# Moving the last head's output weights behind most of its V, and aligning the load buffers to 512 bytes, in a decode attention and MLP kernel

## The chip, the cores and the metric

The kernel runs on one core of a Trainium2 chip. The metric is the device time of one execution in microseconds (us). The profile's own span is 1.8 us shorter than the time (201.4 us for a run of 203.22 before). All runs quoted are at a granted TensorE clock of 1.00.

## The reference, cut to what matters

One token passes through layernorm, grouped-query attention over a cache of 16,384 keys, a residual, and an MLP. With one token there is almost no arithmetic; nearly all the work is reading the caches and weights, 79 MB (before, the load queue takes 96.2% of the DMA engines' time).

```python
# D = 512; Hq, Hkv, Sk, Dh = 32, 8, 16384, 128; everything bf16
h   = x + attention(layernorm(x), k_cache, v_cache, wq, wo)  # K and V: 33.6 MB each; wq and wo: 4.2 MB each
x1  = layernorm(h)        # B's first half adds nothing: its shifts leave only padding for a single position
out = h + x1 + gelu(layernorm(x1) @ w3) @ w4                 # w3 and w4: 1.8 MB each
```

## The kernel before

For each of the 8 KV heads, SyncE (SP) issues two K halves (2 MB), wo (512 KB) and four V quarters (1 MB). VectorE transposes K; TensorE computes scores, the softmax denominator, PV (the softmax weights times V) and the projection with wo; after the last head the MLP runs. All large loads go through one queue, issued in program order. A load waits at the issuing engine until its buffer is free, and everything behind it waits too: in the trace of before nothing is issued from 156.4 to 175.28 us, while wo waits.

```python
sb = lambda name, shape, dt: ctx.enter_context(nc.sbuf_tensor(name, shape, dt))
...                                             # some 25 small tensors, then the load buffers
wo_sb = sb("wo_sb", [128, REP, D], BF16)        # so this one starts at byte 22304 of a partition, 32 mod 256
w3_sb = ...; w4_sb = ...; wq_sb = ...           # all sizes are multiples of 512 bytes:
kraw  = [sb(f"kraw{i}", [128, HALF], BF16) for i in range(NKR)]   # every buffer behind wo_sb starts
vslot = [sb(f"vslot{a}", [128, QTR], BF16)[:, :] for a in range(NQ)]  # at 32 mod 256 as well
...
def load_v(g, a):       # free once PV of quarter a of the head before is done
    P.dma("sp", vslot[a], src, P.at(f"pv{a}", g - 1), sig=f"v{a}")
def load_wo(g):         # free once the projection of the head before is done
    P.dma("sp", wo_sb[:, :, :], wo_in[:, REP * g:REP * (g + 1), :], P.at("proj", g - 1), sig="wo")
...
for g in range(G):
    if g + 1 < G:
        load_k(g + 1, 0)
        load_k(g + 1, 1)
    load_wo(g)
    for a in range(NQ):
        load_v(g, a)
    ...
# behind the last head: w3, then w4 in four pieces
t_w3 = P.dma("sp", w3_sb[:, :, :], w3_in, sig="w3")
t_w4 = [P.dma("sp", w4_sb[:, m0:m1, :], w4_in[:, m0:m1, :], ...) for m0, m1 in W4_CUTS]
```

A load becomes packets of one contiguous run per partition: 16 KB for K, 32 KB for wq, 8 KB for V, 14 KB for w3, 1 KB for wo and w4 (in the trace of before 2,048 packets of 16 KB, 128 of 32, 4,096 of 8, 128 of 14 and 5,888 of 1). They are spread over 16 DMA engines, 768 packets an engine on average (12,288 in all).

The softmax here doesn't subtract the row's maximum and nothing guards it: scores larger than these inputs give would overflow.

## Time and profile before

| | before |
|---|---|
| time, median of 3 (range) | 203.35 us (203.06 to 203.5) |
| HBM read | 79.17 MB, 393 GB/s over the span |
| DMA engines' share, q1 | 96.2% |
| VectorE busy | 124.7 us (62%) |
| one head, from one head's last V landing to the next's | 21.28 us |

The page of the profile, its slices (40 equal parts of the span: the DMA engines' busy tenths, and what they moved) and its queue lines (packets, MB, share of 16 engines' time):

```profile
DMA  6998999999999999999999999999999999099993
GB/s 221 462 462 364 436 433 384 415 441 423 386 419 441 423 397 415 418 434 423 395 421 433 436 384 421 434 434 384 421 431 433 394 415 405 29 360 423 436 351 100
...
q1 hardware_dynamic: 13288, 79.17, 96.2%
q8 instruction: 4, 0.07, 0.1%
...
HBM read 79.17 MB, written 0.00 MB: 393 GB/s over the span
```

The DMA engines are at 9 tenths nearly throughout, but slice 35 moves only 29 GB/s. The next view gives stretches of the trace: the first is steady work, the second the hole. The last two columns are the DMA share and GB/s.

```profile
core 0: us, PE busy (x) PEld busy (x) DVE busy (x) ACT busy (x) POOL busy (x), PEclk, DMA share, GB/s
96.00:160.00 64.00, 26.51 (x822) 24.99 (x822) 44.66 (x13) 3.86 (x27) 0.00 (x0) 1.00 1.02 419
171.00:176.60 5.60, 3.83 (x130) 3.65 (x128) 1.45 (x3) 0.00 (x0) 0.00 (x0) 1.00 0.13 35
```

In the steady stretch the DMA engines are always busy (1.02; the records of packets overlap a little, with 16.2 in flight on average) at 419 GB/s. In the hole they are at 0.13. The time line of the issuing engine shows why (start, duration, engine, line, what; "x4" are four issues in a row):

```profile
154.43 1.94 SPq L71 DMA_DIRECT2D vslot<-in_A_v_cache_dram  x4
175.28 0.38 SPq L71 DMA_DIRECT2D wo_sb<-in_A_wo_dram  x1
175.70 1.93 SPq L71 DMA_DIRECT2D vslot<-in_A_v_cache_dram  x4
```

Nothing is issued between 156.4 and 175.28 us. The time line of TensorE tells what the issue waits for (idle before and its releaser in brackets):

```profile
165.79 1.02 PE L283 MATMUL ot_ps<-p_sb,vslot 128*128 128x4 bf16 x32 [6.43 <-DMA vslot<-in_A_v_cache_dram]
168.27 1.02 PE L283 MATMUL ot_ps<-p_sb,vslot 128*128 128x4 bf16 x32 [1.46 <-DMA vslot<-in_A_v_cache_dram]
170.76 1.01 PE L283 MATMUL ot_ps<-p_sb,vslot 128*128 128x4 bf16 x32 [1.47 <-DMA vslot<-in_A_v_cache_dram]
173.23 1.02 PE L283 MATMUL ot_ps<-p_sb,vslot 128*128 128x4 bf16 x32 [1.46 <-DMA vslot<-in_A_v_cache_dram]
174.56 0.69 PE L290 MATMUL h_ps<-OT,wo_sb 128*128 128x1 bf16 x16 [0.31 <-DVE OT L315]
...
189.01 1.02 PE L283 MATMUL ot_ps<-p_sb,vslot 128*128 128x4 bf16 x32 [1.47 <-DMA vslot<-in_A_v_cache_dram]
```

The four V slots are free after each of the first four groups, at 166.8, 169.3, 171.8 and 174.3 us. But wo stands ahead of them and waits for the projection, which ends at 175.25. The chain that ended last shows the same loop, and the end of the kernel:

```profile
155.93 17.25 DMA vslot<-in_A_v_cache_dram
...
173.23 1.03 PE ot_ps L283 x32
...
174.56 0.70 PE h_ps L290 x16
...
175.28 0.38 SPq L71
...
190.45 8.06 DMA w_sb<-in_B_w_dram
...
198.55 0.41 PE qr_ps L371 x8
...
199.06 0.29 DVE fin L375
```

In the other heads K loads fill the queue meanwhile; the last head has no K to load. After the last V comes the end: w3 and w4 land (the last piece at 198.51 us), and TensorE finishes with it.

Two more readings of the trace, which no view prints, come from its single packet and completion records. (1) From 2 to 171.06 us, 16 packets are in flight without a gap; from 171.06 to 176.54 us, 1.7 on average. (2) A load completes 16 times, and the core has 16 DMA engines: a completion is read here as one engine's, though the records do not name it. The last V of head 6 completes on its first engine at 171.44 us and on its last at 173.18, a spread of 1.74 us. The last V of head 7, behind the hole, completes from 188.51 to 188.96, a spread of 0.45 us.

### The profile page before, as it was taken

What the parts mean: (1) busy time and instruction counts of PE and PEld (TensorE: products, weight loads), DVE (VectorE), ACT (ScalarE), POOL (GpSimd) and SP (SyncE); (2) the same over time, 40 slices, a digit from 0 to 9 for tenths busy, and PEclk for the clock granted to TensorE, in tenths of its full rate; (3) what the DMA queues carried; (4) which work ended last, traced back from release to release, by engine and by line L of the source; (5) the groups of instructions that cost most, each with busy time, mean ns of one, the idle gap of its engine ahead of it and who ended that gap; (6) DMA issues with size and microseconds to landing.
All of it is one profiled execution on the core that took longest, in us unless ns stands there. A gap on an engine that the chain in (4) does not pass through costs nothing.

```text
span 201.4 us, 5325 instructions
## 1 busy us (share of the span) xinstructions
PE 80.3 (40%) x2473; PEld 75.1 (37%) x2473; DVE 124.7 (62%) x69; ACT 17.5 (9%) x85; POOL 0.5 (0%) x5
## 2 busy tenths in 40 slices
PE   0104307344724560467044812491247304664554
PEld 0004206233713550366033802391137303653452
DVE  2186692997399649943995199709990699200030
ACT  2030002000200020002000100002000200040040
POOL 0000000000000000000000000000000000000000
PEclk9999999999999999999999999999999999999999
DMA  6998999999999999999999999999999999099993
GB/s 221 462 462 364 436 433 384 415 441 423 386 419 441 423 397 415 418 434 423 395 421 433 436 384 421 434 434 384 421 431 433 394 415 405 29 360 423 436 351 100
DMA packets 13438, 79.26 MB, mean 394 GB/s; under 512 B 1144, under 2 KB 7032, under 8 KB 7032
## 3 DMA queue, kind: packets, MB, share of 16 engines
q1 hardware_dynamic: 13288, 79.17, 96.2%
q8 instruction: 4, 0.07, 0.1%
q10 hardware_dynamic: 144, 0.00, 0.0%
q14 instruction: 2, 0.02, 0.0%
HBM read 79.17 MB, written 0.00 MB: 393 GB/s over the span
## 4 chain that ended last, share of the span: by engine, by line
DMA 55%; DVE 12%; SPq 12%; PE 11%; issue 7%; ACT 1%; DVEq 0%
DMA vslot<-in_A_v_cache_dram 42%; SPq L71 12%; DVE kt L240 11%; DMA wq_sb<-in_A_wq_dram 8%; DMA w_sb<-in_B_w_dram 4%; PE s_ps L274 4%; PE ot_ps L283 3%; PE h_ps L290 2%; PE q_ps L229 2%; ACT p_sb L263 1%; DVE OT L315 1%; PE den_ps L278 1%; DVE Qbd L251 0%; DVEq L90 0%; PE qr_ps L371 0%
## 5 line engine op out<-in xcount | busy, mean ns | idle before, releaser
L240 DVE STREAM_TRANSPOSE kt<-kraw 128x4096 f32<-128x4096 f32 x16 | 117.5, 7409 | 30.3 <-PE s_ps L274 30.3
L283 PE MATMUL ot_ps<-p_sb,vslot 128*128 128x4 bf16 x1024 | 32.6, 169 | 73.5 <-DMA vslot<-in_A_v_cache_dram 73.5
L283 PEld LDWEIGHTS ot_ps<-p_sb,vslot 128*128 128x128 bf16 x1024 | 29.8, 104 | 76.2 <-DMA vslot<-in_A_v_cache_dram 76.2
L274 PE MATMUL s_ps<-Qcur,kt 128*128 128x16 bf16 x1024 | 28.5, 174 | 8.4 <-DVE kt L240 8.4
L274 PEld LDWEIGHTS s_ps<-Qcur,kt 128*128 128x128 bf16 x1024 | 28.0, 104 | 8.5 <-issue 8.5
L263 ACT ACTIVATE p_sb<-s_ps 128x128 bf16<-128x128 f32 x32 | 8.4, 277 | 146.3 <-PE s_ps L274 146.3
L315 DVE TENSOR_TENSOR OT<-ot_ps,rden 128x4 bf16<-128x4 f32 x8 | 1.3, 163 | 19.1 <-PE ot_ps L283 18.7
L278 PE MATMUL den_ps<-accden,ones_f 128*128 128x4 f32 x16 | 4.5, 349 | 10.6 <-ACT p_sb L263 10.6
L278 PEld LDWEIGHTS den_ps<-accden,ones_f 128*128 128x128 f32 x16 | 4.0, 310 | 11.1 <-issue 11.1
L290 PE MATMUL h_ps<-OT,wo_sb 128*128 128x1 bf16 x128 | 5.5, 173 | 5.7 <-DVE OT L315 5.7
L290 PEld LDWEIGHTS h_ps<-OT,wo_sb 128*128 128x128 bf16 x128 | 4.9, 118 | 6.4 <-DVE OT L315 6.4
L229 PE MATMUL q_ps<-xn,wq_sb 128*128 128x1 bf16 x128 | 3.6, 165 | 8.4 <-DMA wq_sb<-in_A_wq_dram 8.4
L229 PEld LDWEIGHTS q_ps<-xn,wq_sb 128*128 128x128 bf16 x128 | 3.5, 104 | 8.5 <-issue 8.5
L263 ACT ACTIVATION_READ_ACCUMULATOR p_sb<-s_ps 128x1 f32 x32 | 6.6, 207 | 0.0
L314 DVE RECIPROCAL rden<-den_ps 128x4 f32<-128x4 f32 x8 | 1.2, 154 | 6.2 <-PE den_ps L278 6.2
L206 PE MATMUL den_ps<-ln,mean_f 128*128 128x8 f32 x4 | 1.1, 357 | 9.6 <-DVE ln L204 9.0
L206 PEld LDWEIGHTS den_ps<-ln,mean_f 128*128 128x128 f32 x4 | 1.0, 312 | 9.6 <-issue 9.6
L203 DVE CAST ln<-xcol 128x4 f32<-128x4 bf16 x1 | 0.2, 170 | 5.8 <-DMA xcol<-in_A_x_dram 5.8
L257 ACT ACTIVATE Qcur<-Qbd 128x64 bf16<-128x64 bf16 x8 | 2.2, 270 | 11.2 <-DVE Qbd L251 11.2
L375 DVE CAST fin<-qr_ps 128x128 bf16<-128x128 f32 x1 | 0.3, 292 | 4.3 <-PE qr_ps L371 4.3
L371 PE MATMUL qr_ps<-w_sb,hcol 128*1 128x128 bf16 x56 | 2.2, 303 | 0.4 <-DMA w_sb<-in_B_w_dram 0.4
L244 DVE CAST QT<-q_ps 128x32 bf16<-128x32 f32 x1 | 0.2, 192 | 3.2 <-PE q_ps L229 3.2
(52 smaller groups left out, 21.2 us busy)
## 6 DMA issues: line engine op xcount, KB each, us to landing
kraw<-in_A_k_cache_dram SPq DMA_DIRECT2D x16, 2048.0 KB, 18.6
vslot<-in_A_v_cache_dram SPq DMA_DIRECT2D x32, 1024.0 KB, 13.2
wq_sb<-in_A_wq_dram SPq DMA_DIRECT2D x1, 4096.0 KB, 16.7
wo_sb<-in_A_wo_dram SPq DMA_DIRECT2D x8, 512.0 KB, 9.2
w_sb<-in_B_w_dram SPq DMA_DIRECT2D x1, 1792.0 KB, 15.6
w_sb<-in_B_w_dram SPq DMA_DIRECT2D x1, 640.0 KB, 17.0
w_sb<-in_B_w_dram SPq DMA_DIRECT2D x1, 512.0 KB, 18.1
w_sb<-in_B_w_dram SPq DMA_DIRECT2D x1, 384.0 KB, 16.8
```

The costliest lines, as they stand in the source:

```text
L71: self.lists[engine].append((waits, lambda e: e.dma_start(out, in_), (token[0], 16)))
L206: t = P.op(pe, lambda e: e.matmul(den_ps[:, 0:2 * NCH], mean_f[:, :], ln[:, :], start=True, stop=True), t, t_mean, sig="stats")
L229: t_q = P.op("pe", lambda e, h=h, k=k: e.matmul(q_ps[:, h:h + 1], wq_sb[:, k, h * DH:(h + 1) * DH], xn[:, k:k + 1], start=(k == 0), stop=( ...
L240: k_free[n] = P.op("dve", lambda e: e.transpose(dst, src), k_land[n], P.at("qk", g - 1), sig=f"kt{hf}")
L257: P.op("act", lambda e: e.activation(Qcur[:, :], Qbd[:, 64 * g:64 * (g + 1)], ACTF.Copy), t_qbd, P.at("qk", g - 1), sig="qcur")
L263: P.op("act", lambda e, h=h: e.activation(p_sb[:, h * 128:(h + 1) * 128], src[:, h, :], ACTF.Exp, scale=float(SCALE), accum_out=accden[:, ...
L274: P.op("pe_loop", lambda e, J=J, l=lhs, be=be: e.matmul(s_ps[:, 16 * J:16 * J + 16], l, Qcur[:, 16 * be:16 * be + 16], start=(be == 0), st ...
L278: P.op("pe_loop", lambda e: e.matmul(den_ps[:, 0:REP], ones_f[:, :], accden[:, :], start=True, stop=True), "exp", sig="den")
L283: P.op("pe_loop", lambda e, J=J, a=a: e.matmul(ot_ps[:, 0:REP], vslot[a][:, J * DH:(J + 1) * DH], pv[:, J * NQ + a, :], start=(a == 0 and ...
L290: P.op("pe_loop", lambda e, h=h, k=k, l=lhs: e.matmul(h_ps[:, k:k + 1], l, OT[:, h:h + 1], start=False, stop=(h == REP - 1), skip_group_ch ...
L315: P.op("dve", lambda e: e.tensor_tensor(OT[:, :], ot_ps[:, 0:REP], rden[:, :], ALU.mult), P.at("pv3", g), t_rden, P.at("proj", g - 1), sig ...
L371: t = P.op("pe_tail", lambda e, m=m, q=q: e.matmul(row_ps[32 * q:32 * q + 1, 0:128], hcol[:, m:m + 1], w4_sb[:, m, 128 * q:128 * (q + 1)], ...
```

## The change

Two intents: do not let wo of the last head hold up V, and start every load buffer at a multiple of 512 bytes.

```diff
+        big = lambda name, shape, dt: ctx.enter_context(nc.sbuf_tensor(name, shape, dt, align_bytes=512))
...
-        wo_sb = sb("wo_sb", [128, REP, D], BF16)
+        wo_sb = big("wo_sb", [128, REP, D], BF16)
         (the same for w3_sb, w4_sb, wq_sb, kraw and vslot)
...
             if g + 1 < G:
                 load_k(g + 1, 0)
                 load_k(g + 1, 1)
-            load_wo(g)
+                load_wo(g)
             for a in range(NQ):
+                if g == G - 1 and a == NQ - 1:
+                    load_wo(g)
                 load_v(g, a)
```

The first load buffer moves from byte 22304 to 22528 of its partition, the others by the same 224 bytes. On SP wo of the last head moves behind three V quarters. Among the loads nothing else changes. (`kt`, into which VectorE transposes K, lies between these buffers and moves by 224 bytes as well.)

More of the change, by code (lines that the diff above doesn't have):

```diff
@@ L142, in bass_sequential_preLN__gqa_block_cached__mixer_s_mlp__decode_kernel @@
         hcol = sb("hcol", [128, NHC], BF16)
-        wo_sb = sb("wo_sb", [128, REP, D], BF16)
-        w3_sb = sb("w3_sb", [128, NCH, FM], BF16)
-        w4_sb = sb("w4_sb", [128, NHC, D], BF16)
-        wq_sb = sb("wq_sb", [128, NCH, HQ * DH], BF16)
-        kraw = [sb(f"kraw{i}", [128, HALF], BF16) for i in range(NKR)]
+        wo_sb = big("wo_sb", [128, REP, D], BF16)
+        w3_sb = big("w3_sb", [128, NCH, FM], BF16)
+        w4_sb = big("w4_sb", [128, NHC, D], BF16)
+        wq_sb = big("wq_sb", [128, NCH, HQ * DH], BF16)
+        kraw = [big(f"kraw{i}", [128, HALF], BF16) for i in range(NKR)]
         kt = sb("kt", [128, 2 * HALF], BF16)
-        vslot = [sb(f"vslot{a}", [128, QTR], BF16)[:, :] for a in range(NQ)]
+        vslot = [big(f"vslot{a}", [128, QTR], BF16)[:, :] for a in range(NQ)]
         s_ps = ps("s_ps", [128, 512], FP32)
```

## The prediction

> **What bounds the kernel now.** The DMA engines. The page's slices show DMA at 9 tenths in nearly every slice, 79.17 MB read at 393 GB/s over a 201.4 us span; DVE is second (62%, 117.5 us of it transposes). From the trace's packet records, 16 packets (one per DMA engine) are in flight without a break from 2 us to 171.06 us: a head takes 21.27 us. The chain of waits from head 2 on runs through issue, V, PV, OT and projection, but K loads fill the DMA queue meanwhile. The DVE side would allow about 19.4 us per head (transposes end at 172.3, OT waits until 174.3).
>
> The one hole is the last head. It has no K to load, and SP issues in order: wo waits for the projection of head 6 (ends 175.26 in the timeline), and the four V quarters stand behind it, although their slots fall free at 166.8, 169.3, 171.8 and 174.3. The packets show 5.47 us (171.06 to 176.54) at a mean of 1.7 instead of 16 in flight; a slice shows 29 GB/s.
>
> **What the change does, costed.**
> 1. Order. V quarters 0 to 2 of the last head are issued when their slots fall free, V0 some 4 us before the queue runs dry. wo is issued at 175.3 as before, when V2 still has about 3 us of data to go, then V3.  Most engines gain 5.5 us, but landing needs the slowest: three to five of 16 engines lag by up to 1.75 us (each V quarter's 16 completions spread 1.75 us; 16 KB instruction-fetch packets fall among theirs), and today the hole lets them catch up. The last V lands at 188.96. Afterwards, from the last landing of head 6 (173.18) plus wo (32 packets per engine at 47 ns) and V (32 at 312 ns), 11.5 us: 184.7. Gain about 4.3 us.
> 2. All of it is on the critical path: behind the last V stand two nearly equal chains of about 10 us, w3/w4 data (188.96 to 198.51) and PV, projection, layernorm, hidden, row (to about 198.4 without waiting). Both shift.
> 3. Alignment. All loaded buffers now start at 32 mod 256; afterwards at 0. Packets take 312 ns for 8 KB, 612 for 16 KB, 47 for 1 KB[...]. [...] I count 0.4 us.
>
> **Predicted time.** 203.35 - 4.3 - 0.4 = 198.6 us; 80% range 195.3 to 199.8. Faster by over 2% (below 199.3): 0.70; within 2%: 0.29; slower: 0.01.
>
> **What the profile would show.** The low slice near the end gone, packets in flight at 16 until about 193; last V landing at about 184.5; issue-to-landing spread of the last V at 1.7 us instead of 0.45;  Alignment: 8 KB packets at 311 to 312 ns and a head at 21.2 us[...].
>
> **What would make it wrong.** Packets shortened by several ns each (then 194 to 196); or lagging engines deciding more than I think, or the tail not shifting with V (then above 199.5).

The forecast's sum came to 198.6 us: 203.35 less 4.3 for the order and 0.4 for the alignment. The terms behind the 0.4 us, and the packet time and the pace of a head expected if alignment matters, are cut where marked, because no trace or run of this case shows what they rested on.

## The result, and the profile after

| | before | after |
|---|---|---|
| time, median of 4 (range) | 203.36 us (203.06 to 203.5) | 195.24 us (195.15 to 195.33) |
| ratio, 95% interval | | 0.9603 (0.9586 to 0.9619) |
| one head | 21.28 us | 20.90 us |
| last V of head 6 landed | 173.18 us | 170.23 us |
| last V of head 7 landed | 188.96 us | 181.39 us |
| last piece of w4 landed | 198.51 us | 190.42 us |

A ratio is the mean time of one kernel's fast runs over that of the other's fast runs of the same rounds, so it is not quite the ratio of the medians quoted. The kernel is 8.1 us (4.0%) faster. The predicted 198.6 us is 3.4 us too high, and the range, 195.3 to 199.8, is missed by 0.06 us.

The page after, the same parts:

```profile
DMA  6999999999999999999999999999999999999991
GB/s 217 434 434 431 434 417 404 423 432 432 412 422 425 439 431 407 425 451 434 392 430 437 432 414 423 431 451 425 400 429 432 434 408 428 425 429 412 445 368 48
...
q1 hardware_dynamic: 13288, 79.17, 98.1%
...
HBM read 79.17 MB, written 0.00 MB: 410 GB/s over the span
```

No low slice is left before the end. The stretches, at the same times:

```profile
96.00:160.00 64.00, 26.46 (x822) 24.98 (x822) 46.38 (x13) 3.87 (x27) 0.00 (x0) 1.00 1.02 426
171.00:176.60 5.60, 4.47 (x155) 4.29 (x152) 0.16 (x1) 0.78 (x7) 0.00 (x0) 1.00 1.00 417
```

There are two effects. The stretch of the hole is full (0.13 to 1.00). And the steady stretch, where no order changed, moves 426 GB/s in place of 419. Issuing, and the V groups on TensorE:

```profile
151.86 17.37 SPq L71 DMA_DIRECT2D vslot<-in_A_v_cache_dram  x7
172.33 0.38 SPq L71 DMA_DIRECT2D wo_sb<-in_A_wo_dram  x1
172.75 0.51 SPq L71 DMA_DIRECT2D vslot<-in_A_v_cache_dram  x1
```

```profile
177.53 2.70 PE L285 MATMUL ot_ps<-p_sb,vslot 128*128 128x4 bf16 x96
181.44 1.02 PE L285 MATMUL ot_ps<-p_sb,vslot 128*128 128x4 bf16 x32 [1.20 <-DMA vslot<-in_A_v_cache_dram]
```

"x7" at 151.86 are head 6's four V quarters and the first three of head 7. Three V groups of the last head lie ready in one piece (x96) when TensorE comes to them. The chain that ended last, its end:

```profile
153.37 16.86 DMA vslot<-in_A_v_cache_dram
...
183.00 7.41 DMA w_sb<-in_B_w_dram
...
190.46 0.41 PE qr_ps L375 x6
...
190.96 0.29 DVE fin L379
```

The table splits the gain. Up to the last V of head 6, where only the addresses can act, 2.95 us. The last head, 4.62 us more. w3 and w4, 0.52 us more. The packet records show what the addresses do:

```
packets between 54 and 160 us   mean ns (share within 1 ns of the shortest usual duration)
            1 KB (46 ns)    8 KB (309 ns)    16 KB (611 ns)
before      49.0 (57%)      316.6 (5%)       616.0 (6%)
after       46.0 (100%)     309.4 (100%)     611.2 (100%)
```

### The profile page after: what moved, and what is told of

Its sections match the earlier page's. It is cut to its first block, busy times and chain, and to the rows that moved or that the text cites. A ratio compares the mean times of both kernels' runs of the same rounds, so it can differ in the third digit from the quotient of the medians.

```text
span 193.3 us, 5325 instructions
## 1 busy us (share of the span) xinstructions
PE 79.6 (41%) x2473; PEld 74.9 (39%) x2473; DVE 124.9 (65%) x69; ACT 17.5 (9%) x85; POOL 0.5 (0%) x5
## 4 chain that ended last, share of the span: by engine, by line
DMA 47%; DVE 18%; PE 13%; issue 10%; SPq 9%; ACT 1%; DVEq 0%
DMA vslot<-in_A_v_cache_dram 35%; DVE kt L242 16%; SPq L71 9%; DMA wq_sb<-in_A_wq_dram 9%; PE s_ps L276 6%; DMA w_sb<-in_B_w_dram 4%; PE h_ps L292 3%; PE ot_ps L285 2%; PE q_ps L231 2%; ACT p_sb L265 1%; DVE OT L319 1%; PE den_ps L280 1%; DVE Qbd L253 0%; DVEq L90 0%; PE qr_ps L375 0%
```

## The experiments

All gave correct results. Each ran beside the kernel before, whose median was 203.19 to 203.28 us in these rounds.

### The two parts alone

e1 drops the alignment from the changed kernel; e2 drops the order.

```diff
# e1_order_only
-        big = lambda ...: ctx.enter_context(nc.sbuf_tensor(name, shape, dt, align_bytes=512))
+        big = lambda ...: ctx.enter_context(nc.sbuf_tensor(name, shape, dt))
# e2_align_only
-                load_wo(g)                  (and the two lines in the loop over a)
+            load_wo(g)                      (ahead of the loop over a, for every head)
```

> Only the order of the last head's loads changes; the buffers stay at 32 mod 256. Theory A (order and alignment add; order is worth what the slowest DMA engine gains): last V of head 6 lands at 173.2 as before, the last V at about 184.7, time 199.1 us (4.3 less), 8 KB packets mean 316 ns and scattered. Theory B (the order is worth the whole hole of 5.5 us, the alignment only the rest): 197.8 us. Theory C (the order is worth more, nearly all 8.1 us, and the alignment next to nothing): below 197.

> Only the addresses change; wo of the last head stays ahead of all of its V. Theory A: every packet as short as in the changed kernel (309, 611, 46 ns), 20.9 us a head, last V of head 6 lands at 170.2, the hole of about 5.5 us stays, time 199.5 us (3.8 less). Theory B: 200.8 us. Theory C: over 202.5 us.

Measured: e1 198.95 us, ratio 0.9788 (0.9775 to 0.9802), 4.3 us less than before. e2 199.71 us, ratio 0.9826 (0.9812 to 0.9839), 3.5 us less. The stretches of e1 (steady, and the old hole), then of e2 (steady, and its hole, which comes earlier):

```profile
96.00:160.00 64.00, 26.46 (x822) 24.98 (x822) 44.68 (x13) 3.85 (x27) 0.00 (x0) 1.00 1.01 419
171.00:176.60 5.60, 3.81 (x130) 3.62 (x127) 1.48 (x3) 0.00 (x0) 0.00 (x0) 1.00 1.01 420
```

```profile
96.00:160.00 64.00, 26.48 (x822) 24.99 (x822) 46.08 (x13) 3.86 (x27) 0.00 (x0) 1.00 1.01 426
168.00:174.00 6.00, 4.30 (x145) 4.13 (x146) 1.91 (x3) 0.00 (x0) 0.00 (x0) 1.00 0.16 60
```

e1 fills the hole and stays at 419 GB/s. e2 reaches 426 GB/s and keeps a hole (0.16; in its packet records 5.58 us with 1.9 in flight). Theory A holds; B and C fall. The two gains add to 7.8 us of the 8.1. The traces show 0.2 us of the missing 0.3: the order brings the last V forward by 5.58 us on its first engine without the alignment (before to e1) and by 5.59 us with it (e2 to the changed kernel), but on its last engine by 4.25 and 4.45 us, because the engines then land 1.79 us apart in e1 and 1.55 us apart in the changed kernel. Why this lag differs between the two is not known.

e1 also shows why the order is worth 4.3 us and not the 5.5 us of the hole. The last V completes on its first engine at 182.93 us, 5.58 us earlier than before, but on its last engine at 184.71, only 4.25 us earlier. Its spread is 1.79 us, where behind the hole it was 0.45.

### Which alignment counts

Three runs keep the new order and put all load buffers at another offset, by one pad ahead of them.

```diff
# e3_offset64, e5_offset128, e4_offset256: align_bytes dropped, and
+        pad0 = sb("pad0", [128, 144], BF16)     # 176 for 128, 240 for 256
         wo_sb = big("wo_sb", [128, REP, D], BF16)
```

> The changed kernel with every loaded buffer at 64 mod 512 in place of 0, by a pad ahead of them. If what counts is the 32 mod 64 of before (a start inside a 64-byte unit): 195.2 us and packets all 309 and 46 ns. If what counts is a start off a 256-byte boundary[...]: about 199 us, the packets of before (316 and 50 ns).

> The changed kernel with every loaded buffer at 128 mod 512. If any start off a 256-byte boundary costs about the same: 198.5 us, as at 64 (198.57). If the cost falls with the distance, or 128 is the unit that counts: 195.3 us and packets all 309 and 46 ns.

> The changed kernel with every loaded buffer at 256 mod 512. If 64 or 256 bytes are the unit that counts: 195.2 us, all packets 309 and 46 ns. If 512 bytes are: about 199 us.

| run | start of every load buffer | time | ratio (95%) |
|---|---|---|---|
| e1 | 32 mod 256 | 198.95 us | 0.9788 (0.9775 to 0.9802) |
| e3 | 64 mod 512 | 198.57 us | 0.9769 (0.9755 to 0.9782) |
| e5 | 128 mod 512 | 198.41 us | 0.9764 (0.9750 to 0.9777) |
| e4 | 256 mod 512 | 195.34 us | 0.9609 (0.9596 to 0.9622) |
| after | 0 mod 512 | 195.24 us | 0.9603 (0.9586 to 0.9619) |

The steady stretch of e3, then of e4:

```profile
96.00:160.00 64.00, 26.51 (x822) 24.98 (x822) 44.78 (x13) 3.86 (x27) 0.00 (x0) 1.00 1.02 420
```

```profile
96.00:160.00 64.00, 26.45 (x822) 24.96 (x822) 46.13 (x13) 3.85 (x27) 0.00 (x0) 1.00 1.02 427
```

Of the starts tested, only the multiples of 256 bytes are free of the cost. At 64 and 128 nearly the whole cost remains (8 KB packets at a mean of 315.8 ns in both, 316.6 before), at 256 none (309.2 ns, 309.4 after). The 512 of the change is more than is needed. Why 256 is the step is not shown.

### Which buffers, and a cost that depends on what came before

e6 keeps the new order and aligns only V, e7 only wo and w4. Then the converse: e11 aligns all but wq and K, e12 all but V. All by pads.

```diff
# align_bytes dropped in all four; pads in bytes per partition
# e6_v_only:       +224 ahead of vslot
# e7_rows1k_only:  +224 ahead of wo_sb, +288 ahead of w3_sb, +224 ahead of w4_sb, +288 ahead of wq_sb
# e11_k_off:       +224 ahead of wo_sb, +288 ahead of wq_sb, +224 ahead of vslot
# e12_v_off:       +224 ahead of wo_sb, +288 ahead of vslot
```

> The new order with only the four V slots (8 KB packets) at 0 mod 512, all else at 32 mod 256. The V packets' own pace goes from 312.6 to 306.6 ns, 256 of them per engine: 1.5 us below the 198.95 us of the order alone, so 197.4 us; the 1 KB packets stay at 50 ns. (By bytes moved the share would be the same 1.5 us, so this run alone does not tell a cost per packet from one per byte.)

> The new order with only wo and w4 (1 KB packets) at 0 mod 512, all else at 32 mod 256. If a misaligned start costs each packet some ns whatever its size: 368 packets per engine at 4.7 ns, 1.2 to 1.7 us, so 197.2 to 197.8 us. If it costs in proportion to bytes (wo and w4 are 6 of 79 MB): 0.3 us, 198.7 us.

Measured: e6 196.81 us, ratio 0.9687 (0.9673 to 0.9700); e7 196.67 us, ratio 0.9679 (0.9666 to 0.9692). Both are faster than expected. wo and w4 are 6 of 79 MB and bring 2.3 us, so the cost does not go by bytes. And the two gains, 2.1 and 2.3 us, together exceed the 3.7 us that aligning everything brings over e1. So the cost is not one that each packet pays by itself either. The packet records show it: in e6 the K packets, still misaligned, are short (99% at 611 ns), and in e7 the first two V quarters of a head are short and the last two are not. This led to theory D, a cost that builds up, against theory E, a cost of each packet; e11 and e12 tell them apart.

> The changed kernel with only wq and the K buffers (32 and 16 KB packets) back at 32 mod 256. Theory D (each misaligned packet leaves a few ns of work behind, which shows only once some 16 to 30 misaligned packets have come in a row on an engine; aligned packets work it off): the 16 K packets of a head between 64 aligned ones stay at 611 ns, time 195.2 to 195.4 us. Theory E (every misaligned packet pays its own few ns where it stands): K packets at 614 to 616 ns, 128 of them at 4.7 ns, 0.6 us: 195.9 us.

> The changed kernel with only the V slots (8 KB packets) back at 32 mod 256. Theory D: in each head the first two quarters of V keep 309 ns, the last two go to about 314, and the aligned K behind them returns to 611 within a few packets: 16 packets a head at 5.5 ns, 0.7 us, so 195.8 to 196.1 us. Theory E: all 32 V packets of a head slow, 256 at 5.5 to 6 ns: 1.4 to 1.5 us, 196.7 us.

Measured: e11 195.32 us, ratio 0.9612 (0.9598 to 0.9625); e12 195.76 us, ratio 0.9633 (0.9620 to 0.9646). In time e11 matches D; e12 lies 0.04 us below D's range and 0.9 us below E's value. The packets of one typical head (the loads near 66 to 86 us, in their order in the queue), as the share within 1 ns of the shortest duration:

```
             K0     K1     wo     V0     V1     V2     V3
e1           11%     4%    56%     5%     9%     5%     2%
e6 (V)      100%   100%    63%    79%   100%    99%   100%
e7 (wo,w4)   14%     2%   100%   100%    97%    17%     1%
e11 (not K) 100%   100%   100%   100%   100%   100%   100%
e12 (not V)  85%   100%   100%   100%   100%    94%    16%
```

Theory E falls. Misaligned K between aligned neighbours costs nothing measurable; misaligned V behind aligned K and wo stays short for three quarters (24 packets an engine) and only the fourth is slow; a first V quarter behind misaligned wo is partly slow although it is aligned itself (e6, V0). So the delay of misaligned packets shows only after a number of them in a row on an engine: about 16 V packets behind aligned wo (e7), 24 V packets (e12), 16 K packets and some 10 rows of wo (e6). Aligned packets between them undo it. In e11 itself the first K loads, which follow the misaligned wq with nothing aligned between, do turn slow (from 27 to 32 us, down to a third at the shortest duration), and the later ones do not (91 to 100% in every half). That much is shown. What the misaligned packets leave behind is not: no record shows it, and it stays open.

### Why some engines lag

The landing of a load needs the slowest of 16 engines, and up to five are late by 0.8 to 1.8 us, as the 16 completions of each load show. In the trace of before, packets of instruction fetches (16 KB on queue 8 at 23.5, 36.0 and 46.4 us, 8 KB on queue 14 at 80.4 and 135.4) come just before another engine joins the late ones: one engine late by over 0.8 us at 32 us, three at 54, four at 91, five at 155. The changed kernel does the same (fetches at 24.0, 36.2, 46.2, 79.3 and 133.5 us; one engine late at 29 us, two at 40, three at 50, four at 82, five at 138). While one of these fetches runs (before: 1.03 to 1.09 us for 16 KB, 0.31 to 0.33 us for 8 KB), 15.1 to 15.2 load packets are in flight on average, where just before and after it there are 16.1 to 16.2: the fetch takes the place of one load packet. This run unrolls TensorE's loop over heads, so that far more instructions are fetched (19 fetches on queue 8 in place of 4).

```diff
# e8_unrolled, from the changed kernel
-            with eng.Fori(STEP, STEP * (G + 1), STEP) as count:
-                P.emit("pe_loop", eng, count)
+            for g in range(G):
+                P.emit("pe_loop", eng, STEP * (g + 1))
```

> The changed kernel with the TensorE's loop over heads unrolled: eight times the loop's instructions have to be fetched, in 16 KB packets through the same DMA engines. If the engines that lag do so because of instruction fetches, about 9 more such packets appear and the spread of a V quarter's 16 completions grows past 1.6 us, or more engines lag; the time grows by what the slowest engine gains in lag, 0 to 2 us (195.2 to 197). If the lag has another cause: the spread stays at 1.6 us with the same number of lagging engines, and the time at 195.2 us.

Measured: 197.91 us, ratio 0.9741 (0.9726 to 0.9756), 2.7 us slower than the changed kernel, more than the 0 to 2 us expected. Its queue line for instruction fetches, to be read beside "4, 0.07" of the page before (the changed kernel has the same 4):

```profile
q8 instruction: 19, 0.31, 0.6%
```

There are 15 more fetches, 14 of them before the last V has landed. The last V completes on its first engine at 179.74 us, as in the changed kernel (179.84), but on its last at 184.30 (181.39): the spread is 4.56 us, in place of 1.55. That lag covers the whole loss. It grows in steps: the spread of a load is at most 1.9 us until 103 us, 3.1 to 3.2 us from 107 us and 4.6 us at 182, as if one engine had been hit once, twice and three times; the records do not name the engine. While the load queue stays full, an engine that falls behind stays behind: in the trace of before, the spread of 1.7 us that the first fetch brings at 29 us is still there at 173 us. Before the change, the hole let the late engines catch up (0.45 us behind it).

### What bounds the end

e9 moves wo behind the last V quarter as well. e10 also loads w4 in contiguous runs of 2 to 5 KB.

```diff
# e9_wo_last, from the changed kernel
             for a in range(NQ):
-                if g == G - 1 and a == NQ - 1:
-                    load_wo(g)
                 load_v(g, a)
+            if g == G - 1:
+                load_wo(g)
# e10_wo_last_w4rows, on top of e9
-        w4_in = B_w4.rearrange("(m d) c -> d m c", d=128)
+        w4_in = B_w4.rearrange("(d m) c -> d m c", d=128)
-                        hid_ps[i][...], w3_sb[:, k, 128 * m:128 * (m + 1)], xc[:, k:k + 1],
+                        hid_ps[i][...], bass.AP(w3_sb, k * FM + m, [[NCH * FM, 128], [NHC, 128]]), xc[:, k:k + 1],
```

> The changed kernel with the last head's wo behind its last quarter of V in place of ahead of it. The last V lands 1.3 us earlier (about 180.1), wo at about 181.4, just as OT is ready, so the compute chain behind V ends up to 1.3 us earlier. If the w3/w4 data bind the end just as much as that chain: 195.2 us, the last piece of w4 lands at 190.4 as before and TensorE waits for it longer. If the compute chain alone binds: 194.0 us.

> As e9, and w4 loaded with 3 to 5 KB contiguous per partition (hidden unit 14p+m on partition p, w3's columns taken with a step of 14) in place of 1 KB rows. w4's 112 packets of 1 KB per engine at 42.4 ns become 32 of 2 to 5 KB: w4 lands about 0.5 us earlier. If the data bind the end: 194.7 us, or less what TensorE loses on weights read with a 28-byte step (56 of them; if each takes twice its 30 ns, that is 1.7 us on a chain with 1.3 us to spare). If the data do not bind: no gain over e9.

Measured: e9 195.18 us, ratio 0.9606 (0.9593 to 0.9619), the same as the changed kernel. The last V landed at 180.11 us, 1.28 us earlier, and the projection starts 1.2 us earlier, yet the end does not move, as the time line of e9 shows:

```profile
181.58 0.67 PE L292 MATMUL h_ps<-OT,wo_sb 128*128 128x1 bf16 x16 [0.41 <-DMA wo_sb<-in_A_wo_dram]
...
190.50 0.38 PE L375 MATMUL qr_ps<-w_sb,hcol 128*1 128x128 bf16 x8 [0.18 <-DMA w_sb<-in_B_w_dram]
```

The last TensorE group still waits for the last piece of w4, which landed at 190.45 us (190.42 in the changed kernel). So the data bind the end.

But the compute chain is close behind. The hidden layer starts only 0.5 us earlier in e9 (first line) than in the changed kernel (second):

```profile
185.86 0.83 PEld L356 LDWEIGHTS s_ps<-xc,w_sb 128*128 128x128 bf16 x28 [2.51 <-DVE xsum L344]
```

```profile
186.36 0.82 PEld L356 LDWEIGHTS s_ps<-xc,w_sb 128*128 128x128 bf16 x28 [1.79 <-DVE xc L339]
```

In the program this group waits for xc, its normalised input, and for w3 alone. In e9 xc was done at 185.09 us and w3 landed at 185.76, so it was w3, although the profile names a VectorE instruction. From there the chain has about 0.8 us to spare in e9, an estimate: the last 50 products take 1.72 us in e10, where nothing holds them up; they start at 188.38 us in e9 and would end at 190.10, but end at 190.88. In the changed kernel they start at 188.87 and end at 190.84, which leaves about 0.3 us.

e10 196.26 us, ratio 0.9665 (0.9651 to 0.9678), slower than e9. w4 landed at 190.07 us, 0.4 us earlier, but the two groups of the hidden layer read their weights with a step of 28 bytes. The first of them, and the end:

```profile
185.85 1.76 PEld L356 LDWEIGHTS s_ps<-xc,w_sb 128*128 128x128 bf16 x28 [2.52 <-DVE xsum L344]
...
192.06 0.29 DVE L379 CAST fin<-qr_ps 128x128 bf16<-128x128 f32 x1 [6.07 <-PE qr_ps L375]
```

28 weight loads take 1.76 us (63 ns each) where the changed kernel needs 0.82 (29 ns), twice; the 1.9 us more than use up what was spare, and the chain binds instead: the end comes 1.06 us later than in e9 (191.00). Why the step costs this is not shown. No version here beats the changed kernel: e9 is equal to it.

## Why the prediction was wrong

"Faster by over 2%" was right, with 0.70. The number was not: 8.1 us gained in place of 4.8. The verdict owes its clear margin to the alignment, which the prediction hardly counted: the order alone (e1) came to 0.9788 (0.9775 to 0.9802), which leaves 2% open.

1. What bounds the kernel (the DMA queue, one hole in the last head): right. e1 filled the hole and moved nothing else.
2. The order, "gain about 4.3 us": right, 4.3 us in e1. So was the reason that it is less than the 5.5 us of the hole: the last V lands with a spread of 1.55 us after the change (1.7 predicted), and e8 shows that instruction fetches make that lag.
3. "All of it is on the critical path", with two nearly equal chains behind the last V: it is on the path, since the w3 and w4 data shift with V. "Nearly equal" holds too: e9 shows that the data bind, and in the changed kernel the compute chain would have ended only about 0.3 us earlier.
4. Alignment, "I count 0.4 us": this is the step that failed. It was worth 3.7 us (198.95 in e1 to 195.24). The 0.4 us was the author's estimate, with no trace or run of this case behind it: the prediction expected 8 KB packets to stay at 311 to 312 ns. Measured, 8 KB packets shrank by a mean of 7.2 ns, 16 KB by 4.8 and 1 KB by 3.0. (These are durations, and the records of packets overlap a little; the prediction's 312 ns is a pace, from one packet to the next. At that pace the V quarters, 8 packets an engine, followed each other by 2.49 us before and 2.455 after, 312 and 307 ns. So about 5 ns of the pace went, where the prediction expected at most 1.) The trace of before even held a hint: K packets of the same misaligned buffer mostly took 611 ns in the first 25 us (291 of 324) and 613 to 621 ns later (93% from 50 us on), so part of their time was not fixed.
5. "What would make it wrong: packets shortened by several ns each (then 194 to 196)": this is what happened, and the time fell in that band. The stated range, 195.3 at the low end, gave it too little room.

## What to carry to other kernels

Where a queue of loads is the bottleneck, look at its order at the place where the filler runs out: a load that waits for a late event must not stand ahead of loads whose buffers are free (4.3 us here, e1). Try DMA buffers at multiples of 256 bytes: the small tensors ahead of them shifted all of them here, for 1.8% of the time (3.7 us, e1 to after), and 256 mod 512 did as well as 0 (195.34 and 195.24 us). With the queue full no late DMA engine caught up here (a spread of 1.7 us at 29 and at 173 us, 0.45 us behind the hole), so count what a hole hides before you book its whole length as gain: the hole of 5.5 us brought 4.3.
